# Linear attention and two expert layers on one core: a new order of issue in both phases of the first layer

## The chip, the cores and the metric

The kernel runs on one core of a Trainium2 chip. The metric is the device time of one execution in microseconds (us), the median of several runs. PE is TensorE, DVE is VectorE, ACT is ScalarE, POOL is GpSimd, and SP is SyncE, which here only issues DMAs.

## What is computed

The inputs are q, k and v of 8 batches, 8 heads, 576 positions and 64 columns, all in float32. Attention has no softmax: k and v are contracted to a 64 x 64 matrix per head, q is multiplied by it, and each row is divided by its root mean square. Then come two layers of matrix products on 4608 tokens:

```python
kv = np.einsum('bhsd,bhse->bhde', k, v)
out = np.einsum('bhsd,bhde->bhse', q, kv)
out = out / np.sqrt(np.mean(out * out, axis=-1, keepdims=True) + 1e-06) * g_norm
x = out.transpose(0, 2, 1, 3).reshape(4608, 512)
h = x @ moe_w_in            # 512 -> 2048
x = (h * np.cos(h)) @ moe_w_out   # 2048 -> 512
h = ((x @ w1) * (x @ w2)) @ w3    # 512 -> 1024 -> 1024
result = h @ w_out          # 1024 -> 512
```

## The kernel before

**Products.** Every float32 operand is split into a high part, made by ACT, and a low part, the rest, made by DVE or GpSimd (`split`, L120). A product is three matmuls: high by high, high by low, low by high. The weights arrive as 64-bit words and are converted to float32: one operation on ACT and four on DVE per 512 KB piece (`Chunk.convert`, L146). A converted piece is either used or stored to a scratch tensor in HBM for a later phase (L208).

**First phase, steps.** The 4608 tokens are 9 blocks of 512, and w_in is 16 column blocks. A step n is one block of tokens t by one column block m, 144 steps in all, in the order of `steps`: 8 of block 0, 16 of block 1, the other 8 of block 0, then block 2, then the pairs 3 and 4, 5 and 6, 7 and 8 in the same way. Steps 0 to 7 are in `first_steps`, the rest in the loop of `phases` (L1320). Step n emits the 12 matmuls of h for step n + 1 (`emit_h`, L889) and then computes g = h cos(h) of step n in four operations: r on ACT (L1373), u = h / 2pi - r on DVE (L1374), Sin on ACT (L1376), the multiply with h on DVE (L1377). The multiply is the last reader of h's PSUM bank; four banks take turns. When a pair of blocks has its g for two columns, `form` (L834) makes four sums of quarter blocks on POOL (ta, tb: L850 to L853) and asks for their stores to HBM: the raw quarters one step later, ta three and tb four steps later (L856, L857, L861). The u, ta and tb tiles take slots from one list, `spare`; a slot is put back when its store is issued. There are ten slots, two of them (g0, g1) only up to step 112.

**Attention in between.** The half batches u = 6 to 15 are worked on beside the steps. `plan_unit` (L738) puts their pieces into a table with a step and one of four places in it ("top", "pe", "mid", "end"); `starts` (L1328) has the first step of each. A unit loads key and value (`load_kv`, 512 KB each) and query, contracts, multiplies, squares, and then takes its norm (`norms_of`, L711): the sums of squares from PE, copied by ACT and stored to HBM, loaded back in another layout (rsx), a Newton iteration of ten DVE operations (L362 to L378), stored and loaded back as a broadcast (bc), and a multiply on POOL (`emit_x`, L396). `split_x` then splits the rows for h. Units 4 and 5 are in `plan_first`.

**Words in between.** `plan_words` (L755) loads a piece of w_out at the end of step n, starts the conversion two steps later and stores the result at the top of step n + 5; `words` (L1342) has the steps.

**Second phase, parts.** The product with w_out is done by a scheme of seven products per pair of blocks, on sums of quarter blocks; 63 parts of 24 matmuls with 512 columns (the seven of block 2: 48 with 256). The weights' sums (w_left) are made from w_out loaded back: `left_plain` (four pieces, in steps 124 to 133) and `left_sums` (four rounds: steps 137 and 142, parts 2 and 3), each of which asks for its own loads into two buffers called g0 and g1. A part's right side is 1 MB in two halves: `load_right` fetches it from HBM into one of two pairs of raw buffers, `split_right` splits it into one of three x tiles, `part` multiplies. Beside the parts the words of the second layer's weights are loaded, converted and stored, one per part, from part 4 to 44.

**What sets the order.** Steps and parts run under a manual schedule: each engine executes what it is given in the order in which the code emits it, and each DMA of this stretch is issued by SP, in order. An instruction that waits holds all that is behind it on its engine. The third phase (the second layer) is ordered by the scheduler of the framework; the change doesn't touch its code.

Of the kernel before, what the change touches and what calls it, by code (L numbers as in the profile page):

```python
# [13 lines left out]
P = 128  # L14
# [19 lines left out]
def kernel(  # L34
# [313 lines left out]
    def emit_rs(u):  # L348

        m = ap.tile([P, HALF], F32, tag="tmp", bufs=5, name=f"ms_sb_{u}")  # L350
        nc.scalar.activation(m, ms.pop(u)[:, 0:HALF], AF.Copy)
        x = ap.tile([P, RS], F32, tag="rsx", bufs=2, name=f"rsx_{u}")
# [31 lines left out]
    def emit_bc(u):  # L384
        y = rs.pop(u)
        d = dram.tile([2 * NPAIR, HALF], F32, tag="rsd", bufs=2, name=f"rsd_{u}")
        queue(u).dma_start(out=d.rearrange("h s -> (h s)").rearrange("(p f) -> p f", f=RS), in_=y)
        t = ap.tile([P, NPAIR, HALF], F32, tag="bc", name=f"bc_{u}")
        rows = d.rearrange("(p h) s -> h p s", h=2)
        for h in range(2):  # L390
            queue(u).dma_start(out=t[64 * h:64 * h + 64], in_=rows[h].partition_broadcast(64))
        bc[u] = t
# [318 lines left out]
    def norms_of(u, n, newton, x):  # L711
        at(n, "pe", emit_ms, u)
        at(n + 1, "mid", emit_rs, u)
        at(newton, "mid", emit_newton, u)
        at(newton, "mid", emit_bc, u)
        for p in range(NPAIR):
            at(x, "top", emit_x, u, p)
        return x

    def plan_first(n):  # L720

        a, b = 2 * NHALF, 2 * NHALF + 1
# [12 lines left out]
        at(n + 5, "end", load_pairs, b, 1)  # L735
        return {a: norms_of(a, n + 9, n + 13, n + 17), b: norms_of(b, n + 12, n + 17, n + 21)}

    def plan_unit(u, n):  # L738
# [14 lines left out]
        return norms_of(u, n + 13, n + 18, n + 22)  # L753

    def plan_words(i, n):  # L755
# [78 lines left out]
    def form(k, kp, n):  # L834
# [30 lines left out]
        lag = 3 if n < len(steps) - 4 else 2  # L865
# [70 lines left out]

    def left_plain(kk):
        h = slice(0, DM // 2)
        left(0, kk, left_raw(kk, 0)[:, :, h])
        left(1, kk, left_raw(kk, 1)[:, :, h])  # L940

    def left_sums(kk):
        f0, f1 = left_raw(kk, 0), left_raw(kk, 1)
# [376 lines left out]
    def phases():  # L1320
# [7 lines left out]
        starts = (15, 22, 30, 39, 48, 55, 62, 77, 85, 93)  # L1328
        for u, n in zip(range(6, NU), starts):
            ready[u] = plan_unit(u, n)  # L1330
        for u in range(NHALF + 1, NU):
            for t in range(2, NB):
                if u * HALF < (t + 1) * TB and (u + 1) * HALF > t * TB:
                    free = HM + HM + 2 if t == 2 else end_of[t - 3]
# [14 lines left out]
        at(134, "mid", split_right, 0)  # L1349
        at(135, "end", load_right, 2)  # L1350
        at(137, "mid", left_sums, 0)
        at(139, "mid", split_right, 1)
        at(142, "mid", left_sums, 1)

        def do(n, where):
            for f in plan.pop((n, where), ()):
                f()

        do(HM - 1, "end")
        for n in range(HM, NS):  # L1360
# [17 lines left out]
            if m % 2 == 1:  # L1378
                for k, ts in enumerate(TS):
                    if t in ts and all((b, m // 2) in u_of for b in ts):  # L1380
                        form(k, m // 2, n)
            do(n, "end")
        state["conv"] = state["put"] = state["load"]
# [4 lines left out]
        for i in range(n_parts):  # L1388
# [5 lines left out]
            if i + 1 < n_parts and i > 0:  # L1394
                split_right(i + 1)
            if i + 3 < n_parts:
                load_right(i + 3)
            if state["conv"] > state["put"]:
                put(1)
            if state["conv"] < state["load"]:  # L1400
                convert(1)
            if 4 <= i and state["load"] < len(chunks):
                prefetch(state["load"] + 1)
            part(i)
            if 2 <= i < 4:
                left_sums(i)
# [220 lines left out]
```

## Time and profile before

| | us |
|---|---|
| median of 3 runs | 1662.36 (1662.15 to 1665.51) |
| profiled execution | 1660.05 |
| its span, first to last instruction | 1658.3 |
| PE busy | 1490.9 (90%) |
| DVE busy | 1009.5 (61%) |
| ACT busy | 711.9 (43%) |
| POOL busy | 619.9 (37%) |

The profile is of one execution. A line of it names the engine, the source line, the operation and the tiles as out<-in. The shares of busy time are means over stages with different limits, so each stage has to be read by itself. The stages are: start and first steps to 77 us, steps 8 to 143 from there to 594.6 us, parts from 610.6 to 1055 us, the second layer from there to the end. A number in brackets behind an instruction is the idle time of its engine before it, and after the arrow stands what ended it.

### The profile page before, as it was taken

Reading aid. Unit: us, or ns where it says so; the run is one execution under the profiler, and the core shown is the slowest. Engines: PE = TensorE matmul, PEld = TensorE weight load, DVE = VectorE, ACT = ScalarE, POOL = GpSimd, SP = SyncE. Lnnn points to the kernel's source line nnn. Section 1 sums busy time; section 2 is a strip of 40 time slices with the busy share of each in tenths; the row PEclk is TensorE's granted clock in tenths of the full one; section 3 lists DMA queues with packets and bytes.
Section 4 is the critical chain, followed back from the end, with each engine's and each line's share of the span. In section 5 each row is a group of like instructions: output and inputs, shape, how many; then the busy total and the mean of one; then the engine's idle time right before and its main releaser. Section 6 shows DMA issues by size and latency. Waiting matters only on the chain.

```text
span 1658.3 us, 21411 instructions
## 1 busy us (share of the span) xinstructions
PE 1490.9 (90%) x7672; PEld 1261.6 (76%) x7672; DVE 1009.5 (61%) x1533; ACT 711.9 (43%) x1360; POOL 619.9 (37%) x459
## 2 busy tenths in 40 slices
PE   8998889889978755798888799999999999999998
PEld 6776667677757544588666688789999998999997
DVE  4797675585675553667777644485555455555544
ACT  4566554545534432444343344354334334333331
POOL 0054743564363150112111124365554425434430
PEclk8999998999999868899999999999999999999999
DMA  8366864755676664688777777611212122333312
GB/s 322 103 214 189 275 188 145 260 197 194 226 237 233 216 225 143 236 298 287 275 264 282 253 270 237 236 39 67 74 64 77 41 87 83 121 115 108 102 64 83
DMA packets 143915, 295.62 MB, mean 178 GB/s; under 512 B 16480, under 2 KB 50368, under 8 KB 143808
## 3 DMA queue, kind: packets, MB, share of 16 engines
q1 hardware_dynamic: 143104, 293.66, 51.8%
q8 instruction: 60, 0.98, 0.2%
q10 hardware_dynamic: 704, 0.59, 0.1%
q14 instruction: 47, 0.39, 0.1%
HBM read 184.92 MB, written 109.27 MB: 177 GB/s over the span
## 4 chain that ended last, share of the span: by engine, by line
PE 50%; DVE 22%; DMA 13%; issue 6%; ACT 5%; SPq 3%; POOL 2%; DVEq 0%; ACTq 0%; POOLq 0%
PE X L1225 12%; PE V L1225 6%; PE X L1007 5%; DVE g_hl L124 4%; PE o L886 4%; PE o L885 4%; PE o L887 4%; PE V L1007 3%; PE Y L1225 3%; DVE u L1374 2%; DMA a_w<-in_w3t_dram 2%; DVE u L1377 2%; PE h L885 2%; PE h L886 2%; PE h L887 2%
## 5 line engine op out<-in xcount | busy, mean ns | idle before, releaser
L1007 PE MATMUL X<-g_hl,wl 128*128 128x512 f32 (+1 forms) x960 | 223.9, 394 | 68.8 <-ACT g_hl L122 22.0
L885 PE MATMUL h<-x,w_in 128*128 128x512 f32 x576 | 239.9, 416 | 35.6 <-DVE u L1377 35.2
L1007 PEld LDWEIGHTS X<-g_hl,wl 128*128 128x128 f32 x960 | 180.4, 203 | 110.3 <-DVE g_hl L124 24.6
L886 PE MATMUL h<-x,w_in 128*128 128x512 f32 x576 | 231.7, 402 | 2.0 <-DVE x L124 2.0
L887 PE MATMUL h<-x,w_in 128*128 128x512 f32 x576 | 230.8, 401 | 0.0
L1225 PE MATMUL X<-xc,w 128*128 128x384 f32 x1152 | 225.3, 336 | 3.0 <-ACT s L1233 1.7
L124 POOL TENSOR_TENSOR xc<-x2r,xc 128x768 fp32r<-128x768 f32 x70 | 134.9, 1936 | 228.9 <-ACT xc L122 215.5
L1225 PEld LDWEIGHTS X<-xc,w 128*128 128x128 f32 x1152 | 203.0, 188 | 10.8 <-ACT s L1233 3.2
L124 POOL TENSOR_TENSOR g_hl<-g_raw,g_hl 128x1024 fp32r<-128x1024 f32 x31 | 82.4, 2658 | 325.5 <-ACT g_hl L122 287.8
L124 DVE TENSOR_TENSOR g_hl<-g_raw,g_hl 128x1024 fp32r<-128x1024 f32 x95 | 155.1, 1666 | 37.0 <-ACT g_hl L122 36.6
L885 PEld LDWEIGHTS h<-x,w_in 128*128 128x128 f32 x576 | 112.3, 195 | 70.7 <-DVE u L1377 43.1
L1377 DVE TENSOR_TENSOR u<-u,h 128x512 f32<-128x512 f32 x136 | 92.9, 683 | 66.4 <-ACT u L1376 66.0
L122 ACT ACTIVATE g_hl<-g_raw 128x1024 fp32r<-128x1024 f32 x126 | 126.3, 1051 | 15.2 <-DMA g_raw<-g 13.6
L1233 ACT ACTIVATE s<-X 128x384 f32<-128x384 f32 x144 | 66.6, 488 | 152.4 <-PE X L1225 152.1
L886 PEld LDWEIGHTS h<-x,w_in 128*128 128x128 f32 x576 | 112.5, 195 | 25.4 <-DVE x L124 4.1
L887 PEld LDWEIGHTS h<-x,w_in 128*128 128x128 f32 x576 | 111.9, 194 | 25.2 <-DVE w_in L124 0.3
L1376 ACT ACTIVATE u<-u 128x512 f32<-128x512 f32 x136 | 85.5, 629 | 103.9 <-DVE u L1374 103.1
L1374 DVE SCALAR_TENSOR_TENSOR u<-h,r 128x512 f32<-128x512 f32 x136 | 93.1, 685 | 42.1 <-ACT r L1373 31.5
L1225 PE MATMUL V<-xc,w 128*128 128x384 f32 x576 | 116.2, 335 | 0.0
L886 PE MATMUL o<-wchl,ab 128*128 128x512 f32 x288 | 113.0, 392 | 0.0
L885 PE MATMUL o<-wchl,ab 128*128 128x512 f32 x288 | 112.3, 391 | 0.7 <-DVE part L1316 0.5
L887 PE MATMUL o<-wchl,ab 128*128 128x512 f32 x288 | 110.5, 393 | 0.0
(182 smaller groups left out, 2576.6 us busy)
## 6 DMA issues: line engine op xcount, KB each, us to landing
g_raw<-g SPq DMA_DIRECT2D x126, 512.0 KB
x2r<-x_all SPq DMA_DIRECT2D x44, 384.0 KB
kvraw<-in_kv_main_dram SPq DMA_DIRECT2D x32, 512.0 KB
g<-ta SPq DMA_DIRECT2D x32, 512.0 KB
g<-tb SPq DMA_DIRECT2D x32, 512.0 KB
g<-u SPq DMA_DIRECT2D x28, 512.0 KB
g<-u SPq DMA_DIRECT2D x40, 256.0 KB
part<-o SPq DMA_DIRECT2D x36, 256.0 KB
```

The costliest lines, as they stand in the source:

```text
L122: hi = nc.scalar.activation(dst[:, 0], src, AF.Copy)
L124: lo = lo_engine.tensor_tensor(dst[:, 1], src, f32(dst[:, 0]), ALU.subtract)
L885: nc.tensor.matmul(ps, w[0], x[0], start=first, stop=False)
L886: nc.tensor.matmul(ps, w[0], x[1], start=False, stop=False)
L887: return nc.tensor.matmul(ps, w[1], x[0], start=False, stop=last).ins
L1007: nc.tensor.matmul(ps, w[:, a, i2, ws], g[:, b, q], start=first and half == 0 and q == 0 and n == 0, stop=last and final and q == KH - 1 a ...
L1225: nc.tensor.matmul(ps, w[:, self.i, a, k], x[:, b, k], start=first and k == 0 and n == 0, stop=last and k == 1 and n == 2, skip_group_chec ...
L1233: copied.append(nc.scalar.activation(s, ps, AF.Copy).ins)
L1374: nc.vector.scalar_tensor_tensor(u, h_ps[n], INV_2PI, r, ALU.mult, ALU.subtract)
L1376: nc.scalar.activation(u, u, AF.Sin, bias=HALF_PI, scale=TWO_PI)
L1377: nc.vector.tensor_tensor(u, u, h_ps.pop(n), ALU.mult)
```

## The change

The diff moves work in the order of issue and adds no arithmetic.

- The second half of g (Sin, multiply, and `form` behind it) of step n is emitted in step n + 1, behind r and u of that step and ahead of its "mid" work (`g_end`).
- `emit_rs` and `emit_bc` are cut up: the copy, `store_ms`, `load_rs`, the Newton iteration, `store_rs` and `load_bc` each have a step of their own. Units 9 to 15 have a further step between some of these (`late`).
- Key, value and query loads are put at the top of their step instead of its end; seven of the ten units start one or two steps sooner.
- Words: fifteen of the sixteen loads are asked for one to three steps sooner, the conversion starts four steps behind the load instead of two, and the store follows at n + 8 instead of n + 5.
- The loads of `left_plain` and `left_sums` are asked for ahead (`left_load`).
- Parts: splits two parts ahead instead of one, right loads four ahead instead of three, up to two words loaded ahead of the conversion, which starts at part 6.
- The tb and ta stores in the last 32 steps use the short lag.

```diff
+    def store_ms(u):
         d = dram.tile([2 * NPAIR, HALF], F32, tag="msd", bufs=2, name=f"msd_{u}")
         rows = d.rearrange("(p h) s -> h p s", h=2)
         for h in range(2):
-            queue(u).dma_start(out=rows[h], in_=m[h:P:32])
-        queue(u).dma_start(out=x, in_=d.rearrange("h s -> (h s)").rearrange("(p f) -> p f", f=RS))
+            nc.sync.dma_start(out=rows[h], in_=rs[u][h:P:32])
+        rs[u] = d
+
+    def load_rs(u):
+        x = ap.tile([P, RS], F32, tag="rsx", bufs=2, name=f"rsx_{u}")
+        nc.sync.dma_start(
+            out=x, in_=rs[u].rearrange("h s -> (h s)").rearrange("(p f) -> p f", f=RS)
+        )
...
-    def norms_of(u, n, newton, x):
+    def norms_of(u, n, late=0):
         at(n, "pe", emit_ms, u)
         at(n + 1, "mid", emit_rs, u)
-        at(newton, "mid", emit_newton, u)
-        at(newton, "mid", emit_bc, u)
+        at(n + 1 + late, "end", store_ms, u)
+        at(n + 2 + late, "end", load_rs, u)
+        n += 5 + late
+        at(n, "mid", emit_newton, u)
+        at(n + late, "end", store_rs, u)
+        at(n + 1 + late, "end", load_bc, u)
+        n += 4 + late
         for p in range(NPAIR):
-            at(x, "top", emit_x, u, p)
-        return x
+            at(n, "top", emit_x, u, p)
+        return n
...
                 if p == 0:
-                    at(m, "end", load_rest, b)
-                at(m, "end", load_kv, b, p)
+                    at(m, "top", load_rest, b)
+                at(m, "top", load_kv, b, p)
...
-            at(m, "end", load_q, u, p)
+            at(m, "top", load_q, u, p)
...
-        at(n + 2, "mid", begin)
-        at(n + 3, "mid", two)
-        at(n + 4, "mid", two)
-        at(n + 5, "top", done)
+        at(n + 4, "mid", begin)
+        at(n + 5, "mid", two)
+        at(n + 6, "mid", two)
+        at(n + 8, "top", done)
...
-        lag = 3 if n < len(steps) - 4 else 2
+        lag = 3 if n < len(steps) - 2 * NM else 2
...
+    def left_load(kk):
+        lefts["at"] = left_raw(kk, 0), left_raw(kk, 1)
...
     def left_sums(kk):
-        f0, f1 = left_raw(kk, 0), left_raw(kk, 1)
+        f0, f1 = lefts.pop("at")
...
-        starts = (15, 22, 30, 39, 48, 55, 62, 77, 85, 93)
+        starts = (15, 22, 29, 38, 46, 53, 60, 77, 84, 91)
         for u, n in zip(range(6, NU), starts):
-            ready[u] = plan_unit(u, n)
+            ready[u] = plan_unit(u, n, u > 8)
...
-        words = (24, 39, 42, 56, 72, 75, 78, 81, 94, 97, 100, 103, 106, 109, 112, 115)
+        words = (24, 38, 41, 55, 69, 72, 75, 78, 93, 96, 99, 102, 105, 108, 111, 114)
...
         for kk in range(4):
-            at(124 + 3 * kk, "mid", left_plain, kk)
+            at(121 + 4 * kk, "top", left_load, kk)
+            at(124 + 4 * kk, "mid", left_plain, kk)
...
-        at(137, "mid", left_sums, 0)
-        at(139, "mid", split_right, 1)
-        at(142, "mid", left_sums, 1)
+        at(137, "top", left_load, 0)
+        at(139, "mid", left_sums, 0)
+        at(140, "top", left_load, 1)
+        at(141, "mid", split_right, 1)
+        at(142, "end", load_right, 3)
+        at(143, "mid", left_sums, 1)
...
+            if n > HM:
+                g_end(n - 1, n)
             do(n, "mid")
-            nc.scalar.activation(u, u, AF.Sin, bias=HALF_PI, scale=TWO_PI)
-            nc.vector.tensor_tensor(u, u, h_ps.pop(n), ALU.mult)
...
             do(n, "end")
+        g_end(NS - 1, NS)
...
-            if i + 1 < n_parts and i > 0:
-                split_right(i + 1)
-            if i + 3 < n_parts:
-                load_right(i + 3)
+            if i + 2 < n_parts:
+                split_right(i + 2)
+            if i + 4 < n_parts:
+                load_right(i + 4)
             if state["conv"] > state["put"]:
                 put(1)
-            if state["conv"] < state["load"]:
+            if 6 <= i and state["conv"] < state["load"]:
                 convert(1)
-            if 4 <= i and state["load"] < len(chunks):
-                prefetch(state["load"] + 1)
+            if 4 <= i:
+                prefetch(min(state["conv"] + 2, len(chunks)))
             part(i)
-            if 2 <= i < 4:
-                left_sums(i)
+            if 0 < i < 4:
+                if i > 1:
+                    left_sums(i)
+                if i < 3:
+                    left_load(1 + i)
```

## Rows read from the trace of the kernel before

**Rows 1.** Stages: us; busy PE, PEld, DVE, ACT, POOL; PEclk, DMA share, GB/s.
```profile
77.00:500.00 423.00, 376.66 (x2033) 292.08 (x2031) 298.13 (x556) 221.34 (x519) 225.18 (x216) 0.96 0.64 213
500.00:594.60 94.60, 76.17 (x312) 61.05 (x312) 56.26 (x88) 44.13 (x78) 32.64 (x25) 0.91 0.62 220
594.60:610.60 16.00, 0.00 (x0) 0.00 (x1) 6.74 (x11) 4.04 (x7) 5.34 (x6) 0.65 0.61 215
610.60:674.70 64.10, 41.14 (x144) 32.09 (x145) 26.60 (x30) 17.36 (x23) 11.88 (x6) 0.77 0.49 159
674.70:952.00 277.30, 232.77 (x1105) 191.92 (x1104) 199.20 (x234) 112.05 (x146) 52.20 (x20) 0.95 0.79 277
952.00:1658.30 706.30, 695.08 (x3504) 628.82 (x3504) 374.03 (x504) 272.48 (x492) 290.41 (x174) 1.00 0.32 110
```

**Rows 2.** PE's waits, 77 to 500 us: total us, times, longest.
```profile
PE kv L272 <- DMA kvraw<-in_kv_main_dram: 22.7, 7, 10.2
PE h L885 <- DVE u L1377: 15.6, 10, 3.1
```

**Rows 3.** Waits of SP's queue, 77 to 500 us.
```profile
SPq L387 <- DVE rs L368: 55.6, 10, 15.6
```

**Rows 4.** The chain that ended last, 225 to 255 us: start, us, what.
```profile
241.53 1.52 DMA rsd<-rs
...
245.07 6.27 DMA kvraw<-in_kv_main_dram
```

**Rows 5.** ACT in order of time: start, us, operation; in brackets its idle time.
```profile
383.81 0.66 ACT L152 ACTIVATE u_f<-u_w 128x512 f32<-128x512 f32 x1 [5.96 <-DMA u_w<-in_w1pair_dram]
384.37 0.61 ACT L1376 ACTIVATE u<-u 128x512 f32<-128x512 f32 x1
...
541.72 0.63 ACT L122 ACTIVATE wl<-w_out 128x512 fp32r<-128x512 f32 x1 [8.73 <-DMA w_out<-w_out]
...
637.76 0.63 ACT L122 ACTIVATE wl<-w_out 128x512 fp32r<-128x512 f32 x1 [10.70 <-DMA w_out<-w_out]
...
645.18 0.63 ACT L122 ACTIVATE wl<-w_out 128x512 fp32r<-128x512 f32 x1 [1.44 <-DVE w_out L953]
```

**Rows 6.** PE's waits, 500 to 612 us, then 612 to 676 us.
```profile
PE h L885 <- DVE u L1377: 19.6, 5, 8.0
PE X L1007 <- issue: 16.0, 1, 16.0
...
PE X L1007 <- ACT g_hl L122: 22.0, 2, 11.5
```

**Rows 7.** PE's waits, 676 to 952 us.
```profile
PE X L1007 <- DVE g_hl L124: 19.9, 7, 4.1
```

**Rows 8.** DVE, SP and ACT in order of time, a pair of parts at 860 us.
```profile
860.38 3.41 DVE L124 TENSOR_TENSOR g_hl<-g_raw,g_hl 128x1024 fp32r<-128x1024 f32 x1
...
865.14 0.42 SPq L143 DMA_DIRECT2D a_w<-in_w3t_dram  x1
...
866.11 2.35 DVE L124 TENSOR_TENSOR g_hl<-g_raw,g_hl 128x1024 fp32r<-128x1024 f32 x2
...
872.20 0.66 ACT L152 ACTIVATE a_f<-a_w 128x512 f32<-128x512 f32 x1 [5.52 <-DMA a_w<-in_w3t_dram]
```

**Rows 9.** DVE in order of time, steps with nothing but g.
```profile
516.16 0.69 DVE L1377 TENSOR_TENSOR u<-u,h 128x512 f32<-128x512 f32 x1 [0.70 <-ACT u L1376]
...
518.14 0.69 DVE L1377 TENSOR_TENSOR u<-u,h 128x512 f32<-128x512 f32 x1 [0.70 <-ACT u L1376]
```

**Rows 10.** Eight steps as in rows 1; two parts on the chain that ended last.
```profile
503.98:525.80 21.82, 21.82 (x98) 18.04 (x97) 14.63 (x26) 10.59 (x20) 9.94 (x8) 1.00 0.46 161
...
985.01 10.88 PE Y L1007 x48
```

**Rows 11.** Stretches of the pair of parts at 870 us, columns as in rows 1.
```profile
868.00:876.00 8.00, 7.03 (x32) 5.47 (x30) 3.46 (x6) 2.56 (x3) 1.10 (x1) 1.00 1.00 365
876.00:880.00 4.00, 1.43 (x5) 1.15 (x6) 3.22 (x3) 1.43 (x2) 1.44 (x1) 0.89 0.43 117
```

More of the change, by code (lines that the diff above doesn't have):

```diff
@@ L351, in emit_rs @@
         nc.scalar.activation(m, ms.pop(u)[:, 0:HALF], AF.Copy)
-        x = ap.tile([P, RS], F32, tag="rsx", bufs=2, name=f"rsx_{u}")
+        rs[u] = m
+    def store_ms(u):
         d = dram.tile([2 * NPAIR, HALF], F32, tag="msd", bufs=2, name=f"msd_{u}")
@@ L382, with store_rs, load_bc @@
     bc = {}
-    def emit_bc(u):
-        y = rs.pop(u)
+    def store_rs(u):
         d = dram.tile([2 * NPAIR, HALF], F32, tag="rsd", bufs=2, name=f"rsd_{u}")
-        queue(u).dma_start(out=d.rearrange("h s -> (h s)").rearrange("(p f) -> p f", f=RS), in_=y)
+        nc.sync.dma_start(
+            out=d.rearrange("h s -> (h s)").rearrange("(p f) -> p f", f=RS), in_=rs[u]
+        )
+        rs[u] = d
+    def load_bc(u):
+        rows = rs.pop(u).rearrange("(p h) s -> h p s", h=2)
         t = ap.tile([P, NPAIR, HALF], F32, tag="bc", name=f"bc_{u}")
-        rows = d.rearrange("(p h) s -> h p s", h=2)
         for h in range(2):
-            queue(u).dma_start(out=t[64 * h:64 * h + 64], in_=rows[h].partition_broadcast(64))
+            nc.sync.dma_start(out=t[64 * h:64 * h + 64], in_=rows[h].partition_broadcast(64))
         bc[u] = t
@@ L735, in plan_first, with plan_unit @@
         at(n + 5, "end", load_pairs, b, 1)
-        return {a: norms_of(a, n + 9, n + 13, n + 17), b: norms_of(b, n + 12, n + 17, n + 21)}
-    def plan_unit(u, n):
+        return {a: norms_of(a, n + 9), b: norms_of(b, n + 12)}
+    def plan_unit(u, n, late):
         b, half = divmod(u, NHALF)
@@ L752, in plan_unit @@
             at(m + 6, "mid", take_out, u, p)
-        return norms_of(u, n + 13, n + 18, n + 22)
+        return norms_of(u, n + 13, late)
     def plan_words(i, n):
@@ L935, in left @@
         w_left[l, kk] = t
+    lefts = {}
+    def left_load(kk):
+        lefts["at"] = left_raw(kk, 0), left_raw(kk, 1)
     def left_plain(kk):
         h = slice(0, DM // 2)
-        left(0, kk, left_raw(kk, 0)[:, :, h])
-        left(1, kk, left_raw(kk, 1)[:, :, h])
+        f0, f1 = lefts.pop("at")
+        left(0, kk, f0[:, :, h])
+        left(1, kk, f1[:, :, h])
     def left_sums(kk):
-        f0, f1 = left_raw(kk, 0), left_raw(kk, 1)
+        f0, f1 = lefts.pop("at")
         h = DM // 2
@@ L1333, in phases @@
                 if u * HALF < (t + 1) * TB and (u + 1) * HALF > t * TB:
-                    free = HM + HM + 2 if t == 2 else end_of[t - 3]
+                    free = HM + HM + 1 if t == 2 else end_of[t - 3]
                     n = max(ready.get(u, 0), free) + 1
@@ L1345, in phases @@
         for kk in range(4):
-            at(124 + 3 * kk, "mid", left_plain, kk)
+            at(121 + 4 * kk, "top", left_load, kk)
+            at(124 + 4 * kk, "mid", left_plain, kk)
         at(126, "end", load_right, 0)
         at(130, "end", load_right, 1)
-        at(134, "mid", split_right, 0)
-        at(135, "end", load_right, 2)
-        at(137, "mid", left_sums, 0)
-        at(139, "mid", split_right, 1)
-        at(142, "mid", left_sums, 1)
+        at(133, "mid", split_right, 0)
+        at(134, "end", load_right, 2)
+        at(137, "top", left_load, 0)
[4 more added lines that the diff above has]
+        at(143, "mid", left_sums, 1)
         def do(n, where):
@@ L1357, in do, with g_end, seen @@
                 f()
+        def g_end(n, now):
+            t, m = steps[n]
+            u = u_of[t, m // 2][0][:, m % 2]
+            nc.scalar.activation(u, u, AF.Sin, bias=HALF_PI, scale=TWO_PI)
+            nc.vector.tensor_tensor(u, u, h_ps.pop(n), ALU.mult)
+            if m % 2 == 1:
+                for k, ts in enumerate(TS):
+                    if t in ts and all(seen(b, m // 2, n) for b in ts):
+                        form(k, m // 2, now)
+        order_of = {s: i for i, s in enumerate(steps)}
+        def seen(b, kp, n):
+            return order_of[b, 2 * kp + 1] <= n
         do(HM - 1, "end")
@@ L1374, in phases @@
             nc.vector.scalar_tensor_tensor(u, h_ps[n], INV_2PI, r, ALU.mult, ALU.subtract)
+            if n > HM:
+                g_end(n - 1, n)
             do(n, "mid")
-            nc.scalar.activation(u, u, AF.Sin, bias=HALF_PI, scale=TWO_PI)
-            nc.vector.tensor_tensor(u, u, h_ps.pop(n), ALU.mult)
[L1378 to L1381, printed above, removed]
             do(n, "end")
+        g_end(NS - 1, NS)
         state["conv"] = state["put"] = state["load"]
```

## The prediction, made before the changed kernel ran

> **What bounds the kernel now.** I read the stages first [rows 1]: each row gives the length of a stretch, then the busy time of TensorE (PE), its weight loads, VectorE (DVE), ScalarE (ACT) and GpSimd (POOL), the mean granted clock and the DMA share. From 952 us to the end PE is busy nearly all the time, so a looser order ahead of it can't shorten that. Between 77 and 952 us it can: PE stands still for 423.00 - 376.66 = 46.3 us in the first stage, 18.4 in the second, 16.0 between 594.6 and 610.6 (no matmul at all), 23.0 in 610.6 to 674.7 and 44.5 in 674.7 to 952, 148 in all. The clock adds to that: means of 0.96, 0.91, 0.77 and 0.95 say that part of these stretches ran at the lower level (1.2 GHz); the mean is lowest, 0.65, in the stretch without a matmul, and 1.00 from 952 on, where PE hardly pauses.
>
> Next, who ends PE's waits. In the first stage it is the key and value loads (22.7 us in 7 waits) and the bank of an h that the last multiply of a step, L1377, gives back (15.6 in 10) [rows 2]. Neither is short of an engine; both are an order. The loads are late because SyncE's queue stands: 55.6 us behind the Newton result [rows 3]. The worst case reads in two rows [rows 4]: the norm's store goes out at 241.53, the key load that stands behind it in the queue at 245.07, and it takes 6.27 us. The bank is late because ACT stands in front of a word load: at 383.81 it had been idle 5.96 us, and Sin, next in its queue, waits too [rows 5]. The same group shows it for the loads of the second phase's weights: 8.73 and 10.70 us idle. In the second stage PE's 19.6 us go to L1377 again, and part 0 waits 16.0 for a bank whose multiply stands behind such weight sums; then 22.0 for splits queued behind the next ones [rows 6]. In 674.7 to 952 the waits are for the split of the very part that comes next (19.9 of the 44.5 on X alone) [rows 7].
>
> **The change, term A: 77 to 500 us.** Key, query and rest loads go from the end of a step to its top, and no DMA of the norm chain is any longer asked for in the step that makes its data: the msd store, rsx load, rsd store and bc load each get a step of their own. A load then waits behind about one step of SP's queue, not behind a landing. The kv matmuls are issued two steps later, behind the h of a third: 3 x 2.73 = 8.2 us against the 6.27 that the load takes [rows 4, 10]. Words get four steps from load to first use instead of two: 4 x 2.73 = 10.9 us against 7.06 us from issue (865.14) to use (872.20) in a busier stretch [rows 8, 10]. A step's floor of 2.73 us is 21.82 us for eight [rows 10]. I also count what is added. DMAs moved: per unit two msd stores, one rsx, one rsd, two bc; per word load one load and one store; they are no more than before and pass only SP's queue. g's second half now stands behind the next step's first half on ACT and DVE. That takes away the ping-pong: a step costs DVE 518.14 - 516.16 = 1.98 us now with 0.70 of it idle [rows 9], and would cost about 1.3. It takes from the bank: four h banks give 3 x 2.73 = 8.2 us until one is needed again; today r, u, Sin and multiply (0.61 for Sin [rows 5], 0.69 for the multiply [rows 9], the other two alike: 2.6) leave 5.6 of cover, afterwards one step more is used and about 3.3 is left. While that cover holds it costs nothing. GpSimd's sums (form) now stand in front of the same step's query splits, not behind; I charge 3 us for late query splits. Of 38.3 us of waits I take 30 back, and 9 of the up to 0.04 x 423 = 17 us of clock, less 3: **-36 us**. Bounds: -15 (only word waits go) and -52 (46.3 idle and part of the clock).
>
> **Term B: 500 to 674.7 us.** 26 steps of 2.73 and six parts of 5.44 (10.88 for two [rows 10]) are 103.6 us of the 174.7. What stays: four rounds of left_sums, each 645.81 - 637.76 = 8.05 us of ACT and DVE in turn [rows 5], no longer with the DMA wait in front. By hand: the round in step 139 overruns the cover by about 4 us. The round in step 143 now stands in front of step 143's own second half, so part 0 waits 6 us for one bank and 7 for the other. The fourth round can't be asked for until the third has freed both g homes; its load (7 us, as above) and the five until the piece that part 5 reads make 13, and the split behind it 3. Together 33, plus 3 for slots: 140 us. That would be -35; I take **-32**. Bounds: -12 (if the last two rounds wait for DMA as now) and -50 (if parts hide half of the rest).
>
> **Term C: 674.7 to 952 us, 39 parts.** split_right and load_right run one part further ahead (two instead of one, four instead of three), and word loads two ahead. The third x home was idle; now a split waits until the part before the current one has ended, and then has a whole spare part. Today both splits of a pair are bunched: DMA is at 1.00 for eight microseconds while they load and at 0.43 once loads wait for raw buffers [rows 11]. The raw buffers stay two deep, so this loop remains: split, then load into the freed half. Floors: PE 39 x 5.44 = 212 us; DMA 0.79 x 277.3 = 219 us if it never paused; DVE 199 us of work [rows 1]. I don't expect the DMA floor, as the loop still makes it pause; nor today's 277, as ACT's wait for the word (5.52 us [rows 8]) and the split just in time go. I take 245, a little under the middle (248): **-32**. Bounds: -8 (the loop of two buffers is the limit) and -58 (DMA floor).
>
> On this loop the Trainium skill (DMA: Bandwidth & Descriptors, Bandwidth) has 1 MB landing in 6.15 us. By that the loads would land well inside two parts, and C would be near -45 by an estimate from that page. The rows of this case show over 7 us for half a megabyte among other traffic, so I keep -32.
>
> **Rest.** The split of the clock after 952 and the third phase: 0, within 4 us either way, since PE is busy there. Two words finish one part later; under 2 us, inside C.
>
> **Sum.** The profiled execution took 1660.05 us, with 1658.3 of span. 1660.05 - 36 - 32 - 32 = 1560; the median of the runs is 2.3 above the profiled one, so 1562.
>
> **Rivals.** *Two raw buffers still rule phase two* (0.16): C is -8 and its lateness reaches back into the last rounds (B -26). For it: DMA falls to 0.43 once loads stand before raw buffers [rows 11]. Against: the wait for a word is as long as a part (5.52 against 5.44). 1660 - 70 + 2 = 1592.
>
> *All waits go* (0.15): A -46, B -42, C -52, 1522. For it: the causes are orders, not work. Against: left_sums stays serial.
>
> *DVE held by GpSimd* (0.08): a DVE split of 1024 columns takes 3.41 us beside a GpSimd split and 2.35 / 2 = 1.18 without [rows 8]. The sums of form on GpSimd now start just ahead of a step's x splits and words on DVE. The 40 forms, if each holds one DVE operation for 2.2 us, are 88 us of DVE time; with a sixth of it beyond the cover A loses 15: 1577. The Trainium skill (SBUF - State Buffer, Who interferes with whom) states this as an exclusive lock between GpSimd and a DVE instruction with two SBUF inputs; the trace agrees (3.41 against 1.18).
>
> *Slots run short in the last block* (0.07): from step 112 there are 8 slots for u, ta and tb, and a step's delay uses the last. A u slot is then reused one step (2.73 us) after its store was asked for, and 512 KB take about 6 [rows 4]: about 3 us in each of six forms, 18 us, and B falls to -12: 1582.
>
> *Slower* (0.07): the second half a step later gives each h bank back too late. It decides where a step's extra work on ACT and DVE exceeds the 3.3 us of cover. With 1.0 us more in each of the 136 steps from 8 on, 136 - 100 = +36: 1698. Even 0.74 us a step eats the whole gain. Against it: DVE is busy 298 of 423 us there.
>
> *Nothing changes* (0.03): the queues wait for the same landings elsewhere; 1662.
>
> **How the numbers follow.** The forecast has 0.44, and 1540 to 1585 as its own stretch. The range 1518 to 1615 takes in both neighbours and leaves out the slower case, the null and the far ends of A to C, about 0.2. A difference of 0.2% (3.3 us) is about what can be told from no change: faster 0.44 + 0.16 + 0.15 + 0.08 + 0.07 = 0.90, same 0.03, slower 0.07.
>
> **What would show it.** Right: in the waits of PE, kv on its load falls from 22.7 to under 5, and no ACT wait for word or weight loads above 2 us remains before 500. In parts 6 to 44 the mean falls from 7.1 to 6.3 us with the DMA share above 0.85. Part 0 still waits for a bank. Wrong: PE waits on L1377 in steps with nothing but g (bank), DVE u waiting for a store of g (slots), PE on g_hl splits as often as now with the share at 0.79 (C), or a third phase of another length.

## The result and the profile after

| | before | after |
|---|---|---|
| median of four runs each, us | 1663.07 (1662.15 to 1665.51) | 1546.28 (1545.48 to 1551.26) |
| ratio to before, 95% interval | | 0.930 (0.928 to 0.932) |
| profiled execution, us | 1660.05 | 1545.72 |
| its span, us | 1658.3 | 1543.9 |

The change saves 7.0%, and the time lies inside the range, 16 us below the forecast of 1562. Where it came from is read by stage. Each stage below ends at the same instruction in both traces, so the columns add up to the spans within rounding.

| stage | before | after | difference | forecast |
|---|---|---|---|---|
| start to step 8 | 77.0 | 75.0 | -2.0 | 0 |
| steps 8 to 117 (A) | 424.1 | 405.1 | -19.0 | -36 |
| step 118 to part 5 (B) | 173.6 | 143.0 | -30.6 | -32 |
| parts 6 to 44 (C) | 277.3 | 214.4 | -62.9 | -32 |
| part 45 to the end | 706.2 | 706.4 | +0.2 | 0 |

The total is right partly because two errors cancel: A gave half of what was forecast, C twice as much. That much of it is luck.

The same stages of after, with the columns of [rows 1]: us; busy PE, PEld, DVE, ACT, POOL; PEclk, DMA share, GB/s.

```profile
75.00:480.00 405.00, 375.14 (x2033) 294.76 (x2032) 318.06 (x562) 220.86 (x524) 229.92 (x216) 0.95 0.67 222
480.00:623.00 143.00, 113.88 (x457) 91.10 (x457) 95.97 (x124) 64.71 (x105) 52.54 (x36) 0.88 0.69 241
623.00:837.50 214.50, 214.50 (x1106) 184.49 (x1105) 191.74 (x234) 117.62 (x144) 54.99 (x20) 1.00 1.00 363
837.50:1543.90 706.40, 695.52 (x3505) 630.35 (x3503) 369.03 (x504) 270.60 (x491) 285.08 (x174) 1.00 0.33 109
```

The third row is the plainest: PE is busy in all of its 214.50 us. Nothing is left to win there by order. In the first row PE still stands still for 405.00 - 375.14 = 29.9 us and the mean clock is 0.95, no better than before. DVE is busy 318 us, 20 more than before, although the change adds no arithmetic.

PE's waits of after, 75 to 480 us, then 480 to 623 us (total us, times, longest):

```profile
PE h L903 <- DVE x L124: 8.2, 3, 7.7
PE kv L272 <- DMA kvraw<-in_kv_main_dram: 7.8, 3, 4.3
PE h L902 <- DVE u L1390: 7.5, 4, 4.3
PE out L321 <- POOL qhl L124: 4.4, 4, 1.9
...
PE X L1030 <- DVE u L1390: 10.8, 1, 10.8
PE X L1030 <- ACT wl L122: 6.9, 1, 6.9
PE h L902 <- DVE u L1390: 6.0, 2, 5.2
PE X L1030 <- issue: 3.8, 1, 3.8
```

Against [rows 2], kv fell from 22.7 to 7.8 and the wait for a bank (now the multiply at L1390) from 15.6 to 7.5. What is new is 8.2 us for splits of x and 4.4 for splits of the query. From 623 to 837.5 us PE has no wait.

ACT's waits for the words, first in steps 8 to 117 before, then in parts 6 to 44 before, then in the same parts after:

```profile
ACT u_f L152 <- DMA u_w<-in_w1pair_dram: 33.4, 10, 6.5
```
```profile
ACT a_f L152 <- DMA a_w<-in_w3t_dram: 46.7, 11, 7.0
ACT d_f L152 <- DMA d_w<-in_w12w_dram: 33.0, 10, 6.8
```
```profile
ACT d_f L152 <- DMA d_w<-in_w12w_dram: 11.1, 11, 2.0
ACT a_f L152 <- DMA a_w<-in_w3t_dram: 3.1, 6, 1.1
```

In steps 8 to 117 of after no wait for a word is left. In the parts the words still come last, but by 2.0 us at most, and no longer by 7.

SP's queue, first before (77 to 500 us), then after (75 to 480 us):

```profile
SPq L304 <- POOL qhl L124: 16.0, 7, 5.6
```
```profile
SPq L304 <- POOL qhl L124: 82.1, 23, 9.3
SPq L394 <- DVE rs L376: 27.1, 6, 6.3
```

The wait for the Newton result fell from the 55.6 us of [rows 3] to 27.1. The query load's wait for GpSimd's split, 16.0 us before, is 82.1 now. So the queue stands for another reason, and the experiments begin from there.

### The profile page after: what moved, and what is told of

It is laid out like the page before. It is cut to its first block, busy times and chain, and to the rows that moved or that the text cites. A ratio compares the mean times of both kernels' runs of the same rounds, so it can differ in the third digit from the quotient of the medians.

```text
span 1543.9 us, 21450 instructions
## 1 busy us (share of the span) xinstructions
PE 1465.7 (95%) x7672; PEld 1254.4 (81%) x7672; DVE 1023.1 (66%) x1533; ACT 714.3 (46%) x1360; POOL 624.8 (40%) x459
## 4 chain that ended last, share of the span: by engine, by line
PE 74%; DVE 12%; DMA 6%; issue 3%; ACT 2%; POOL 2%; SPq 1%; DVEq 0%; ACTq 0%; POOLq 0%
PE X L1248 13%; PE X L1030 12%; PE V L1030 6%; PE V L1248 6%; PE h L902 5%; PE h L903 5%; PE h L904 5%; PE o L903 4%; PE o L902 4%; PE o L904 4%; PE Y L1248 3%; PE Y L1030 2%; PE kv L272 2%; DMA kvraw<-in_kv_main_dram 2%; DVE u L1390 1%
## 5 line engine op out<-in xcount | busy, mean ns | idle before, releaser
L1030 PE MATMUL X<-g_hl,wl 128*128 128x512 f32 (+1 forms) x960 | 207.2, 376 | 23.1 <-DVE u L1390 10.8
L1030 PEld LDWEIGHTS X<-g_hl,wl 128*128 128x128 f32 x960 | 171.4, 193 | 56.8 <-DVE u L1390 11.2
L124 POOL TENSOR_TENSOR g_hl<-g_raw,g_hl 128x1024 fp32r<-128x1024 f32 x31 | 82.1, 2648 | 245.5 <-ACT g_hl L122 194.4
L124 DVE TENSOR_TENSOR g_hl<-g_raw,g_hl 128x1024 fp32r<-128x1024 f32 x95 | 124.9, 1342 | 57.4 <-ACT g_hl L122 57.2
L1415 ACT ACTIVATE r<-h 128x512 int32<-128x512 f32 x136 | 81.1, 596 | 150.9 <-PE h L904 150.7
```

The source lines that it names most:

```text
L124: lo = lo_engine.tensor_tensor(dst[:, 1], src, f32(dst[:, 0]), ALU.subtract)
L1030: nc.tensor.matmul(ps, w[:, a, i2, ws], g[:, b, q], start=first and half == 0 and q == 0 and n == 0, stop=last and final and q == KH - 1 a ...
L1415: nc.scalar.activation(r, h_ps[n], AF.Identity, bias=0.25, scale=INV_2PI)
```

## The experiments

The theory at the start: A fell short because the late second half of g brings new waits, and C went further because the words, not the raw buffers, had held the parts. Experiments 1 to 3 ask about C, 4 to 12 about A and B. "Ratio" is to the kernel before on the same chip, with its 95% interval; chips differed between groups of experiments, so kernels are compared by ratio. A point of ratio (0.01) is 16.6 us.

### e1: the split lead undone

```diff
-        at(142, "end", load_right, 3)
...
-            if i + 2 < n_parts:
-                split_right(i + 2)
-            if i + 4 < n_parts:
-                load_right(i + 4)
+            if i + 1 < n_parts and i > 0:
+                split_right(i + 1)
+            if i + 3 < n_parts:
+                load_right(i + 3)
```

> The changed kernel with one thing undone: splits again one part ahead and right loads three ahead; words stay two ahead. Theory (both the split just in time and the wait for the word held parts 6 to 44 at 7.1 us): without the spare part PE waits on a split again in part of the parts, 5.44 goes to about 6.2 us, 39 x 0.75 = 30 us more, near 1575 us. Rival (only ACT's stand for the word mattered): parts stay at 5.44 to 5.6, at most 6 us more, below 1553.

Measured: 1547.39 us, ratio 0.933 (0.931 to 0.936). Parts 6 to 44 (columns as above):

```profile
625.20:840.30 215.10, 214.75 (x1105) 184.38 (x1104) 189.44 (x232) 119.01 (x143) 51.79 (x20) 1.00 0.97 355
```

The rival's range holds: PE still runs almost without a pause. With the words two ahead, splitting two parts ahead and loading four ahead brings at most a microsecond in this stage.

### e2: one word ahead instead of two

```diff
-                prefetch(min(state["conv"] + 2, len(chunks)))
+                prefetch(min(state["conv"] + 1, len(chunks)))
```

> The changed kernel with one thing undone: one word loaded ahead of the conversion instead of two; splits stay two parts ahead. Theory: ACT stands for each word again (5 us), but a split has a whole part of 5.44 us to spare, so parts 6 to 45 go to about 5.9 us, 18 us more, near 1564. Rival (only the words mattered): back to about 6.9 us a part, 55 us more, near 1600.

Measured: 1599.28 us, ratio 0.965 (0.960 to 0.969), 53 us slower than after. The parts, and PE's largest wait in them:

```profile
621.30:891.60 270.30, 225.02 (x1105) 189.69 (x1103) 182.61 (x232) 112.77 (x146) 54.46 (x20) 0.93 0.84 290
```
```profile
PE X L1030 <- ACT s L1049: 38.6, 5, 12.0
```

This is the rival's figure. The stage is back at 270.3 of the 277.3 us of before. The wait is for a bank whose copy (s) stands on ACT behind the conversion of a word that hasn't landed. A word asked for one part ahead has 5.44 us to land and needs longer (7.06 us in [rows 8]); one asked for two parts ahead has 10.88. When ACT waits for it, the copies and the splits behind it wait too, and PE runs at the lower clock beside that (mean 0.93, and 225.0 busy microseconds for the same matmuls instead of 214.5).

### e3: the part loop alone, in the kernel before

The kernel before, with only the changes to the loop over parts (splits, loads, words) and the load of part 3 that they need.

```diff
+        at(142, "end", load_right, 3)
...
-            if state["conv"] < state["load"]:
+            if 6 <= i and state["conv"] < state["load"]:
                 convert(1)
-            if 4 <= i and state["load"] < len(chunks):
-                prefetch(state["load"] + 1)
+            if 4 <= i:
+                prefetch(min(state["conv"] + 2, len(chunks)))
```

> The kernel before with the change of the part loop alone (splits two ahead, right loads four ahead, words two ahead). Theory: the whole 63 us between parts 6 and 45 come from here and nothing that goes before matters to it: 1663 - 63 = 1600, parts at 5.44. Rival (the part loop is fast only because the steps before leave SP's queue empty): half of it, near 1630.

Measured: 1592.39 us, ratio 0.959 (0.958 to 0.961): 68 us, of which parts 6 to 44 give 277.3 - 216.0 = 61.3 and parts 0 to 5 another 6.5. Steps 8 to 117 take 425.4, as before. C stands by itself; it doesn't need the steps' new order.

### e4: the second half of g back in its own step

The change as it is, but with Sin, multiply and sums of step n emitted at the end of step n, behind its "mid" work; the stores come one step sooner with them.

```diff
-            if n > HM:
-                g_end(n - 1, n)
             do(n, "mid")
+            g_end(n, n)
             do(n, "end")
-        g_end(NS - 1, NS)
```

> The changed kernel with the second half of g back in its own step, behind the mid work, with form behind it. Theory (in steps 8 to 117 the gain was only half of that forecast because GpSimd's sums now stand in front of the query splits, which hold the query buffers and with them SP's queue: 82 us of SP's waits on L304, 16 before): SP's wait on the query load falls under 25 us, PE's waits on qhl and kv nearly go, but the ping-pong of ACT and DVE returns; the two cancel, 1546 within 8. Rival (taking the ping-pong away is what gained the 19 us there): near 1566.

Measured: **1521.45 us** (1520.27 to 1522.95), ratio 0.917 (0.916 to 0.918). This is faster than both kernels: by 25 us than after going by the medians, by 22 going by the ratios. Neither expectation held (1546 within 8, or near 1566). Steps 8 to 117 take 386.1 us, 38.0 less than before:

```profile
72.70:458.80 386.10, 367.34 (x2034) 289.29 (x2033) 305.03 (x563) 224.49 (x524) 227.13 (x215) 0.98 0.71 234
```

PE's, SP's and DVE's waits in that stretch:

```profile
PE h L903 <- DVE x L124: 7.9, 5, 5.6
PE h L902 <- DVE u L1390: 4.2, 2, 3.3
PE kv L272 <- DMA kvraw<-in_kv_main_dram: 3.0, 2, 2.4
```
```profile
SPq L304 <- POOL qhl L124: 58.6, 21, 6.2
```
```profile
DVE u L1390 <- ACT u L1389: 27.0, 42, 1.1
DVE u L1416 <- ACT r L1415: 25.0, 26, 1.5
```

Of the 19 us that this stage gains over after, PE's idle time gives 29.9 - 18.8 = 11.1 and its busy time 375.1 - 367.3 = 7.8: the same matmuls, but fewer of them at the lower of the two levels (mean 0.98 against 0.95). Step 118 to part 5 gives another 3.8. The wait of 7.9 us for splits of x stays, so it doesn't belong to the late half. The rows for DVE matter too. The ping-pong between ACT and DVE is back (27.0 us before the multiply), and PE waits for the multiply no longer than in after: DVE waits 57.5 us for r in after, here 52.0 for r and Sin together.

Two paths lead from the late half to PE, and both can be read in the trace of after. GpSimd and the queue of SP around 160 us, then DVE at the end of the same stretch (start, us, what; idle time in brackets):

```profile
159.15 1.48 POOL L867 TENSOR_TENSOR ta<-u,u 128x512 f32<-128x512 f32 x1
160.71 1.36 POOL L868 TENSOR_TENSOR ta<-u,ta 128x512 f32<-128x512 f32 x1
162.02 1.41 POOL L869 TENSOR_TENSOR tb<-u 128x512 f32<-128x512 f32 x1
163.39 1.31 POOL L870 TENSOR_TENSOR tb<-u,ta 128x512 f32<-128x512 f32 x1
164.65 1.25 POOL L124 TENSOR_TENSOR qhl<-q,qhl 128x288 fp32r<-128x288 f32 x1
```
```profile
156.05 0.43 SPq L253 DMA_DIRECT2D kvraw<-in_kv_main_dram  x1
165.93 0.33 SPq L304 DMA_DIRECT2D q<-in_qt_dram  x1
...
166.78 1.51 SPq L873 DMA_DIRECT2D g<-u  x1
```
```profile
172.38 0.69 DVE L1416 SCALAR_TENSOR_TENSOR u<-h,r 128x512 f32<-128x512 f32 x1 [4.74 <-DMA g<-u]
```

Four sums (5.6 us) stand in front of the query's split; the next query load needs the tile that this split frees, so SP issues nothing between 156.5 and 165.9; the store of u stands behind that load; and at 172.38 DVE has waited 4.74 us for the slot that this store gives back. On DVE that is the only such wait in the stage. Most of the waiting for slots in after is GpSimd's, before its sums, 15.3 us in nine waits where e4 has 2.6 in two; the largest row:

```profile
POOL ta L867 <- DMA g<-ta: 9.6, 4, 4.6
```

Experiments 5, 6 and 11 try the two paths one by one and together.

### e5: only the sums go behind the "mid" work

The late half stays as in after; only `form` moves from in front of the "mid" work of its step to behind it, so that GpSimd does the splits first.

```diff
             if n > HM:
-                g_end(n - 1, n)
+                g_end(n - 1)
             do(n, "mid")
+            if n > HM:
+                forms(n - 1, n)
...
```

> The changed kernel with form alone moved behind the mid work of its step, the second half of g still a step late. With the second half back in its own step (form behind the mid work too) the time was 1521, 25 less than 1546. Theory (the cost is GpSimd's order, the four sums in front of the query split): most of the 25 come back, 1521 to 1528. Rival 1 (slots: the sums and their stores still come a step later, so tiles are reused sooner after their stores): stays at 1540 to 1547. Rival 2 (the h bank is given back a step later): stays at 1540 to 1547 as well, with PE's waits on the multiply as before.

Measured: 1535.00 us, ratio 0.926 (0.922 to 0.929). By the medians 11 of the 25 us come back, by the ratios 8, though the interval still overlaps that of after (0.928 to 0.932) a little. In the trace steps 8 to 117 are 7.8 us shorter, and SP's wait for the query split falls from 82.1 to 68.5. So GpSimd's order is a part, and not the whole; none of the three expectations held.

### e6: e4 with the stores of g a step later

```diff
-        at(n + 1, "top", raw)
-        lag = 3 if n < len(steps) - 2 * NM else 2
+        late = n < len(steps) - 2 * NM - 2
+        at(n + 2 if late else n + 1, "top", raw)
+        lag = 4 if late else 2
```

> The second half of g in its own step (1521), and the stores of u, ta and tb each asked for one step later up to step 110, as the changed kernel has them. Theory (GpSimd's order): slots don't matter, 1521 to 1526. Rival 1 (slots): DVE's u and GpSimd's ta wait for stores of g, PE waits on the multiply, and most of the 25 us come, 1538 or more.

Measured: 1537.56 us, ratio 0.926 (0.922 to 0.929), 15 us over e4 by the ratio. DVE's wait for a slot, in e4 and in e6, in the same steps:

```profile
DVE u L1416 <- DMA g<-u: 5.6, 3, 3.9
```
```profile
DVE u L1417 <- DMA g<-u: 24.6, 8, 4.0
```

A store one step later keeps a slot one step longer, and in e4 the slots already ran out three times. In the changed kernel every store comes that much later than in e4, as its second half of g is a step late. But the waits stand elsewhere there (4.7 us on DVE, most on GpSimd), so the 15 us of e6 can't be carried over to it as they are.

### e7 and e8: e4 without the room for the norm, without the room for the words

e7 asks for each DMA of the norm in the step that makes its data, as before. e8 starts the conversion two steps behind the load and stores at n + 5, as before.

```diff
-        at(n + 1 + late, "end", store_ms, u)
-        at(n + 2 + late, "end", load_rs, u)
+        at(n + 1, "mid", store_ms, u)
+        at(n + 1, "mid", load_rs, u)
...
-        at(n + late, "end", store_rs, u)
-        at(n + 1 + late, "end", load_bc, u)
+        at(n, "mid", store_rs, u)
+        at(n, "mid", load_bc, u)
```

> The second half of g in its own step (1521), and the four DMAs of each norm asked for at once behind their producers as before the change; all loads at their new places. Theory (the norm's DMAs held SP's queue and with it the key loads, 22.7 us of PE's waits before, plus clock): about 15 to 25 us more, 1536 to 1546. Rival (the loads at the top of their steps are early enough by themselves): 1521 to 1526.

```diff
-        at(n + 4, "mid", begin)
-        at(n + 5, "mid", two)
-        at(n + 6, "mid", two)
-        at(n + 8, "top", done)
+        at(n + 2, "mid", begin)
+        at(n + 3, "mid", two)
+        at(n + 4, "mid", two)
+        at(n + 5, "top", done)
```

> The second half of g in its own step (1521), and the words of the first phase converted two steps behind their loads and stored at n + 5, as before the change. Theory (ACT's wait for a word held the multiply and its bank: 15.6 us of PE's waits to step 117 and a part of the clock): 12 to 22 us more, 1533 to 1543. Rival (with the queue of SP free the word lands within two steps): 1521 to 1526.

Measured: e7 1538.68 us, ratio 0.928 (0.924 to 0.932); e8 1535.95 us, ratio 0.927 (0.923 to 0.930). Against e4 that is 18 and 16 us by the ratios, both as the theories had it. PE's wait that grew, first e7, then e8:

```profile
PE kv L272 <- DMA kvraw<-in_kv_main_dram: 15.7, 5, 5.9
```
```profile
PE h L902 <- DVE u L1390: 9.5, 7, 4.8
```

In e4 these are 3.0 and 4.2. What stands in front of them, SP's wait in e7, then ACT's and SP's in e8:

```profile
SPq L363 <- DMA msd<-ms_sb: 34.4, 13, 5.3
```
```profile
ACT u_f L152 <- DMA u_w<-in_w1pair_dram: 18.3, 11, 2.9
```
```profile
SPq L208 <- DVE u_f L160: 36.8, 9, 9.1
```

In e4 the first is 14.8 us, and the other two are not there. In e7 it is as the prediction drew it: a norm's landing holds the key load in SP's queue. In e8 a word's landing holds ACT, and with it Sin and a bank, as the prediction had it. But the word's store, asked for at n + 5 again, also stands in SP's queue until the conversion is done. No run parts the two, so the 16 us are the price of both.

### e9 and e10: the gaps that the order by hand leaves

In e4 part 0 waits 7.8 us for a bank whose multiply stands behind the round of `left_sums` in step 143. e9 moves that round behind the steps. e10 adds to e9 a start one step later for the last unit, whose Newton iteration stands in front of the multiply in step 112.

```diff
-        at(143, "mid", left_sums, 1)
+        at(NS, "top", left_sums, 1)
```

> The second half of g in its own step (1521), and the second round of left_sums moved from step 143 to the first part, behind the last multiply of the phase. Theory (part 0 waits 4.0 and 7.8 us for its two banks because this round stands in front of the last multiplies): both waits go, the round of 8 to 11 us runs beside parts 0 and 1, part 2 may wait 2 us for its split; 8 to 12 us less, 1509 to 1513. Rival (the round is serial work that must be done before part 5 in any case): the gain comes back as a wait at part 5, 1518 to 1522.

```diff
-        starts = (15, 22, 29, 38, 46, 53, 60, 77, 84, 91)
+        starts = (15, 22, 29, 38, 46, 53, 60, 77, 84, 92)
```

> The kernel of e9_sums_behind, and half batch 15 started one step later, so that its Newton iteration no longer stands on DVE between the two halves of the x split that step 112 waits for (5.6 us of PE's wait; the eleven Newton operations take 0.18 us alone, but here 1.2 beside GpSimd's sums). Theory: that wait and the clock behind it go, 6 to 9 us less than e9. Rival (DVE held by GpSimd's sums costs the same wherever Newton stands): PE waits on the multiply a step later, within 2 us of e9.

Measured: e9 1522.99 us, ratio 0.918 (0.917 to 0.920); e10 1524.65 us, ratio 0.919 (0.916 to 0.921). Neither differs from e4 by more than the intervals. PE's waits in parts 0 to 5, e4 and then e9:

```profile
PE X L1030 <- DVE u L1390: 7.8, 1, 7.8
PE X L1030 <- ACT wl L122: 7.2, 1, 7.2
PE X L1030 <- DMA g<-tb: 4.0, 1, 4.0
```
```profile
PE X L1030 <- ACT g_hl L122: 8.5, 1, 8.5
PE X L1030 <- ACT wl L122: 6.2, 1, 6.2
PE X L1030 <- DMA g<-tb: 3.1, 1, 3.1
```

The wait for the bank goes, and one of the same size (8.5 us) appears at part 5, for its split, as the rival said; the round is done later by as much. e10 does the same on a small scale: the wait of 4.6 us that e9 has for the split in step 112 goes, and 4.4 us for a bank take its place in step 115.

### e11: both paths mended under the late half

The late half stays; the sums stand behind "mid" as in e5, and the stores are asked for in the same steps as in e4, the raw quarters at the end of that step instead of its top.

```diff
-        at(n + 1, "top", raw)
-        lag = 3 if n < len(steps) - 2 * NM else 2
+        at(n, "end", raw)
+        lag = 2 if n <= len(steps) - 2 * NM else 1
...
-        at(n + lag + (lag > 2), "top", store, 4, tb, tag_b)
+        at(n + lag + (lag > 1), "top", store, 4, tb, tag_b)
```

> The second half of g a step late as in the changed kernel, but with both suspected costs mended: form stands behind the mid work, and the stores of u, ta and tb are asked for as soon as in the kernel with the second half in its own step (1521.5). Theory (the late second half cost its 25 us through GpSimd's order, about 11, and through the slots, about 13, and nothing else): 1519 to 1526. Rival 1 (a part of the cost is the h bank given back a step later): 1530 or more, with PE's waits on the multiply. Rival 2 (without those two costs the missing ping-pong pays): 1516 or less.

Measured: 1529.66 us (1525.78 to 1532.05), ratio 0.922 (0.919 to 0.924). That is 14 us better than after by the ratios, and still 8 over e4, both clear of the intervals; rival 1's "1530 or more" is nearer than the theory's 1519 to 1526. Of the 14 us 5 to 6 come on top of e5, but the intervals of e5 and e11 overlap, so the share of each path is not settled. Together the two paths explain about two thirds of the cost of the late half.

### e12: e4 with the Newton iteration behind the multiply

```diff
-        at(n, "mid", emit_newton, u)
+        at(n, "end", emit_newton, u)
```

> The second half of g in its own step (1521.5), with each Newton iteration at the end of its step, behind the multiply, instead of in the mid work. Theory (DVE held by GpSimd's sums stretches Newton from 2 to 5 to 8 us, and what stands behind it pays: the x split that step 112 waits for, 5.6 us, and multiplies that give banks back): 8 to 14 us less, 1508 to 1514. Rival (the stretch only moves on to the next step's first half): within 3 us of 1521.

Measured: 1537.88 us, ratio 0.926 (0.923 to 0.929), 15 us worse than e4, where the theory had 8 to 14 us less and the rival no change. SP's queue points to the reason:

```profile
SPq L394 <- DVE rs L376: 56.9, 11, 9.7
```

In e4 this is 15.7 us in 5 waits. The result now comes at the very end of its step, and its store, asked for there or a step later, holds SP's queue as in [rows 3]. PE's wait for key loads rises with it, from 3.0 to 7.4 us, and the one for a bank from 4.2 to 10.6.

## Why the prediction was right, and where it wasn't

**A, steps 8 to 117: the mechanisms held, one step failed.** "While that cover holds it costs nothing" and "I charge 3 us for late query splits" priced the late second half of g. By e4 against after it costs 22 to 25 us in the whole, 19 of them in this stage. Without it A is 424.1 - 386.1 = -38.0, close to the forecast of -36. So the mechanisms of norm and words were right, and together with the loads right in size; e7 (18 us) and e8 (16 us) show two of them at work. No run undoes the loads' new places alone. What took half of A back:

- GpSimd's order: the sums ahead of the splits hold the query loads in SP's queue (82.1 us of waits, 68.5 in e5, 58.6 in e4; most of the rise from the 16.0 of before is thus not the late half's). e5 gives 8 to 11 us back. The prediction saw this order and priced only the late split, not the queue behind it.
- The slots: each store a step later. e11 gives 5 to 6 us on top of e5, by itself within the noise; added to e4 alone the same delay costs 15, which is clear of it. The two costs don't simply add up. The prediction had slots as a rival, but only for the last block.
- About 8 us remain between e11 and e4, and their cause stays open. Three things differ there: the raw stores at the end of their step instead of its top, the bank's shorter cover (PE waits 6.7 us for L1390 in e11, 4.2 in e4), and the Newton iteration beside GpSimd's sums (its 132 operations on DVE take 54.2 us in e11, 56.9 in after, 36.5 in e4 and 40.9 before). No run parts the three; e12 moved the iteration, but in e4, and paid for it elsewhere.

The ping-pong of [rows 9], which this edit was to take away, was worth nothing: it is idle time of DVE, and with it back in e4 the stage is shorter. DVE's waits for r only took the place of those for Sin.

The slower rival named the same edit, by way of the h bank, with a price (136 us) that was far too high. PE waits for a bank four times in this stage (7.5 us against 15.6 before), so the cover was used up in a few steps and not in each; most of the cost came by GpSimd, SP's queue and the slots, which that rival did not name.

Of the signs given for A, the words' came true (no wait is left), and the key load's did not: kv fell to 7.8 us and not under 5; in e4 it is 3.0.

**B, step 118 to part 5: right in the sum, near in the pieces, and partly by luck.** Forecast 140 us of 174.7, measured 143.0 of 173.6. The round of sums in step 139 leaves a gap of 5.2 us (forecast 4), part 0 waits 3.8 + 10.8 = 14.6 for its two banks (13), part 5 waits 6.9 for the weights and 1.7 for its split (13 and 3). These waits come to 28.4 us where the forecast had 33; the weights took half of their price. The floor of 103.6 us for the matmuls was 10.3 too low: PE is busy 113.9 us at a mean clock of 0.88, and B had no term for the clock, only 3 us for slots, which held GpSimd (18.2 us in three waits) but hardly DVE (0.4). Order by hand found the right gaps; that the sum came out within 3 us is two errors that cancel. No run undoes an edit of B other than the place of one round (e9), so what each of them is worth stays open.

**C, parts 6 to 44: direction right, size wrong by half.** The step that failed is "The raw buffers stay two deep, so this loop remains: split, then load into the freed half". That loop never held the parts. [rows 11] showed DMA at 0.43 while loads stood before raw buffers, and the prediction took this as a limit; it was slack that the wait for a word had made. e2 puts the word back to one ahead and the 277 us return (270.3); e1 undoes the loads' lead and nothing returns. So what held the parts was ACT's stand at the words, and the forecast set it beside the loop as one limit of two. All of PE's 44.5 us of idle time went, and 232.8 - 214.5 = 18.3 us of busy time that the lower clock had cost (means of 0.95 and 1.00), for which C had no term. PE's floor was what came, past the bound of -58, and the forecast took the middle instead. The floor itself was nearly exact: 39 x 5.44 = 212 against 214.5.

On the transfers the forecast set a floor of 219 us from the share of 0.79. The stage ended 4.5 us under it. Nor does a share of 1.00 tell that the transfers can go no faster. A stretch of this stage of after, with the share as full as in the whole stage at 363 GB/s and in the 365 of [rows 11]:

```profile
660.00:690.00 30.00, 30.00 (x226) 28.87 (x225) 26.16 (x34) 15.76 (x21) 9.76 (x3) 1.00 1.02 398
```

The Trainium skill (DMA: Bandwidth & Descriptors, Bandwidth) names about 358 GB/s for each core when both cores of an HBM domain stream, and measured 425 with one core alone on transfers of 16 MB. This kernel runs on one core, and its 363 and 398 lie between the two figures. So PE is at its end in this stage, and what a shorter matmul would gain there is open; no run tried it.

**Rest: right.** From part 45 on 706.4 against 706.2 us.

**The rivals.** "Two raw buffers" fell with e1 and e2: the buffers were the same in all runs, and PE still ran without a pause in after. "All waits go" was right for C (-62.9, beyond its -52) and, but for the late half, near in A (-38.0 in e4, against its -46). "DVE held by GpSimd" is in the trace, at the Newton iteration and not at the splits for which it was priced; what that costs in time no run shows. "Slots run short in the last block" did not come: DVE waits 0.4 us for a slot in steps 118 to 143.

## What to carry to other kernels

When several things in a loop are late together, ask which single wait, in an engine that works in order, the others stand behind: one word asked for one part sooner was worth 53 us, and the deeper lead of the splits beside it at most one. A piece put a step later isn't free while its engine has time: it also changes the order on the engines behind it, holds its tiles longer and delays their stores, and each of these is to be priced by the queue that it enters. After a change of many edits, undo them one at a time; here the best kernel (1521.45 us) is the change without one of them.

## What the runs showed of the hardware

**Small operations of DVE beside GpSimd.** The Newton iteration of unit 15 in after, DVE and the neighbours on GpSimd (start, us, what):

```profile
455.90 1.19 DVE L374 TENSOR_TENSOR rs<-rsx,rs 128x18 f32<-128x18 f32 x1
457.12 0.18 DVE L375 SCALAR_TENSOR_TENSOR rs<-rs,rs 128x18 f32<-128x18 f32 x1
457.34 0.18 DVE L376 SCALAR_TENSOR_TENSOR rs<-rs,rs 128x18 f32<-128x18 f32 x1
```
```profile
455.80 1.25 POOL L870 TENSOR_TENSOR tb<-u,ta 128x512 f32<-128x512 f32 x1
457.36 1.28 POOL L867 TENSOR_TENSOR ta<-u,u 128x512 f32<-128x512 f32 x1 [0.31 <-DVE rs L375]
```

The operation beside a sum takes 1.19 us and ends with the sum; the two that begin around the 0.3 us in which GpSimd pauses take 0.18. The iteration is eleven operations a unit (the ten counted ahead and the addition in front of them), 132 in steps 8 to 117. In after 89 of them begin while GpSimd has no operation running, and all of these take 0.16 to 0.18 us; 43 begin beside one, and 41 of those end within 0.04 us after it. So an operation on 18 columns can cost more than a free one on 512 (0.69 us): the eleven of this unit take 8.2 us, about 2 if nothing held them. Of the 20 us by which DVE's busy time grew without added work, the iteration is 16 (40.9 to 56.9). The Trainium skill (SBUF — State Buffer, Who interferes with whom) describes the port that the two engines share as an exclusive lock; these rows agree.
